# Changing when a routed-expert kernel loads weights and values, turns its pages, and drains GpSimd

## The chip, the cores and the metric

One core of one Trainium2 chip. The metric is device time in microseconds (us) of one execution. Lower is better. The kernel before takes 331.72 us (median of three runs, 329.25 to 331.78). A difference of 2% is 6.6 us.

Engine names in the profile: PE is TensorE, PEld its weight loads, DVE is VectorE, ACT is ScalarE, POOL is GpSimd, SP the engine that only issues DMAs. A "q" behind the name (POOLq) is that engine's sequencer.

## The reference, cut to what matters

```python
# attention: q, k, v are (8, 8, 576, 64); 128 random features; no softmax matrix
q_p, k_p = phi(q * scale), phi(k * scale)          # phi: projection, minus maximum, exp
num = einsum(q_p, einsum(k_p, v)); den = einsum(q_p, k_p.sum(seq)) + 1e-6
x = (num / den) -> (8, 576, 512)                   # 4608 tokens of 512
# experts: 8 of them, w1 (512 x 1024), w2 (1024 x 512); each token goes to one
e = argmax(x @ w_gate)  or the expert of the token before, by a local gate
out = softmax(x @ w_gate)[e] * (relu(x @ w1[e]) @ w2[e])
```

The tokens of one expert are gathered in pages of 128. There are 38 pages here: 18 for each half ("epoch") of the tokens and two overflow pages.

## The kernel before

Attention runs in 47 pipelined steps. 36 of them handle k, and q follows 11 steps behind. Then the gate makes the lists of tokens of epoch 0, and pages start while the lists of epoch 1 are made. A page is: gather (GpSimd, indirect DMA), turn (transposition, on TensorE or by DMA from SP), w1 matmul, relu, transposition of h, w2 matmul, scaling on VectorE, scatter (GpSimd, indirect DMA). The parts that the change touches:

```python
t_ = dict(k=kp4, v=kp2)[nm].tile(...)                   # two buffers for v
(nc.sync if nm == "v" else nc.gpsimd).dma_start(out=t_[:, :, c], in_=rows[nm][...])
...
def w_load():                                           # 64 loads of 256 KB, in order w1 then w2
    nc.gpsimd.dma_start(out=wdst[l][...], in_=src[e]...)
...
def turn(xg):      nc.sync.dma_start_transpose(out=xt, in_=xg)
def turn_pe(xg):   # four transposes on TensorE, one copy on ScalarE
...
def page(j, nw, gates):
    def mid():                                          # between the two halves of the w1 matmul
        if j + 1 < NEP:
            xts[j + 1] = turn_pe(xgs.pop(j + 1))
    ...  # hidden(j), transposition of h of page j - 1, gather of page j + 5
    if NEP <= j + 3 < NST:
        xts[j + 3] = turn(xgs.pop(j + 3))
    for _ in range(nw):
        w_load()
...
mo2 = pool("mo2", 4, **rw)                              # y: four results may wait for their scatter
```

From page 17 on, 1.5 results per page are multiplied by w2 and scattered.

The softmax here doesn't subtract the row's maximum and nothing guards it: scores larger than these inputs give would overflow.

Of the kernel before, what the change touches and what calls it, by code (L numbers as in the profile page):

```python
# [9 lines left out]
F32 = mybir.dt.float32  # L10
BF = mybir.dt.bfloat16
# [12 lines left out]
NEP = 18  # L24
# [6 lines left out]
def kernel(  # L31
# [12 lines left out]
    nc = tc.nc  # L44
    B, H, S, Dh = q.shape
    M, _ = omega.shape
    D, E = moe_w_gate.shape
    _, _, F = moe_w1.shape
# [3 lines left out]
    NP = B // 2  # L52
    DC, FC = D // 128, F // 128
# [10 lines left out]
    def pool(name, bufs, c=ctx, **kw):  # L64
        return c.enter_context(tc.tile_pool(name=name, bufs=bufs, **kw))
# [15 lines left out]
    kp1, kp2, kp3, kp4, kp6 = [pool("kp%d" % n, n, kctx, side="right") for n in (1, 2, 3, 4, 6)]  # L81
# [4 lines left out]
    LAG = 11  # L86
    NK = 9 * NP
# [5 lines left out]
    def load(P, nm, g):  # L93

        j0, nj = (8 * P, 8) if nm == "q" else (8 * P + 4 * g, 4)
        if nm == "q":
            t_ = arena.rearrange("p a x -> p (a x)").rearrange("p (w j x) -> p w j x", w=2, j=8)[:, P % 2]
        else:
            t_ = dict(k=kp4, v=kp2)[nm].tile([128, nj, 9 * Dh], F32 if nm == "v" else BF, name=nm + "s")
        cuts = [0, 4, 9] if (P, nm, g) == (0, "k", 0) else [0, 9]  # L100
        for c0, c1 in zip(cuts, cuts[1:]):
            c = slice(c0 * Dh, c1 * Dh)
            (nc.sync if nm == "v" else nc.gpsimd).dma_start(out=t_[:, :, c], in_=rows[nm][:, j0:j0 + nj, c])
        stg[P, nm, g] = t_
# [32 lines left out]
    def w_load():  # L137
        if wload and wdst[wload[0][0]] is not None:
            l, e, i = wload.pop(0)
            src = (moe_w1, moe_w2)[l]  # L140
            w = src.shape[2]
            nb = 1024 // w
            nc.gpsimd.dma_start(  # L143
                out=wdst[l][:, ds(e * WE + i * 1024, 1024)].rearrange("p (c f) -> p c f", f=w),
                in_=src[e].rearrange(("(c p) f -> p c f", "(p c) f -> p c f")[l], p=128)[:, i * nb:(i + 1) * nb, :])
# [222 lines left out]
    lists = {}  # L368
# [196 lines left out]
    pages, xgs, xts = [], {}, {}  # L565
# [27 lines left out]
    WH = 17  # L593
    outs, hs, done, spare = [], {}, [], list(range(3, 9))
    NST = 2 * NEP + 2

    def hidden(n, xt, ev_src, mid=lambda: None):
        ev = nc.values_load(ev_src, engines=(PE,), min_val=0, max_val=(E - 1) * WE,
# [12 lines left out]
    def hidden_t(h, n=FC):  # L611

        tp = ps_t.tile([128, FC, 128], BF, name="tp")
        for f in range(n):
            nc.tensor.transpose(tp[:, f], h[:, f], ident_bf)  # L615
        n_ = spare.pop(0) if spare else 0
        ht = arena[:, n_].rearrange("p (f c) -> p f c", c=128) if n_ else moh.tile([128, FC, 128], BF, name="ht")
        nc.vector.tensor_copy(ht[:, 0:n], tp[:, 0:n])  # L618
        if n < FC:
            nc.sync.dma_start_transpose(out=ht[:, n:], in_=h[:, n:].rearrange("p f c -> p (f c)"))  # L620
        return ht, n_
# [33 lines left out]
    def page(j, nw, gates):  # L655
        def mid():

            if j + 1 < NEP:
                xts[j + 1] = turn_pe(xgs.pop(j + 1))

        def gate_part():
            if gates:
                next(ga, None)

        if j < NST:
            hs[j] = hidden(j, xts.pop(j), pages[j][1], mid)
        gate_part()
        if j >= 1:
            h, ev = hs.pop(j - 1)
            done.append((pages[j - 1], hidden_t(h, FC // 2 if NEP <= j < NST - 1 else FC), ev))  # L670
        gate_part()
        if j + 5 == NEP:
            assert 1 in lists
            add_pages(1)
        if j + 6 == 2 * NEP:
            add_overflow()
        if j + 5 < NST:

            gs = pages[j + 5][0]
            xgs[j + 5] = fetch(gs[-1:], xgs.get(j + 5))  # L680
        if 2 * NEP <= j + 6 < NST:
            xgs[j + 6] = fetch(pages[j + 6][0][:1])
        if NEP <= j + 3 < NST:
            xts[j + 3] = turn(xgs.pop(j + 3))
        for _ in range(nw):
            w_load()


    todo = {}

    def at(t, *a):
        todo.setdefault(t, []).append(a)

    at(-1, load, 1, "k", 0)
    at(-1, load, 0, "q", 0)
    for P in range(NP):
        if P + 1 < NP:
            if P:
                at(9 * P - 5, load, P + 1, "k", 0)
            at(9 * P + 5, load, P + 1, "v", 0)  # L700
            at(9 * P - 1, load, P + 1, "k", 1)
            at(9 * P + 9, load, P + 1, "v", 1)
            at(9 * P + LAG + 1, load, P + 1, "q", 0)

    kvg, ga, early = [], None, [0, 0]
    gc = gate_consts()
# [17 lines left out]
    for t in range(NK + LAG + 3):  # L724
        s = t - LAG
        tk, tq, to = t < NK, 0 <= s < NK, 0 <= s - 2 < NK
        P, c = t // 9, t % 9

        slots(tk, tq)
        if tk:  # L730
            pe_kproj(t)
            dve_kmax(t)
        if tq:
            pe_qproj(s)
            act_qexp(s)
        if tk:
            act_kexp(t)
        if 0 <= s - 3 < NK:
            store_x(s - 3)
        if to:  # L740
            pe_o(s - 2)
        if t + 2 < NK + LAG:
            tp = pe_transposes(t + 2, s + 2)
        if t % 9 in (1, 6) and 6 <= t <= NK + 1:
            kvg.append(kv_pieces((t - 6) // 9, int(t % 9 == 1)))
        for g in list(kvg):
            if next(g, 1) == 1:
                kvg.remove(g)
        if to:
            dve_finish(s - 2)  # L750
        if t + 2 < NK + LAG:
            evac(t + 2, tp)
        if len(pages) > 0 and t > early[1] + 1:
            if early[0] == 0:
                xts[0] = turn_pe(xgs.pop(0))
            page(early[0], 1, False)
            early[0] += 1
        if ga is not None:
            next(ga, None)
            if next(ga, 1) == 1:  # L760
                ga = None

        if tk:
            pool_va(t)
        do(t)
        if t in (1, 3, 5, 7):
            next(gc, None)
        if tk:
            for _ in range(t > 8 and t % 5 in (0, 2, 4)):
                w_load()  # L770
        else:
            for _ in range(2 if 0 not in lists else 0):
                w_load()
        if t == NK + 1:

            kctx.close()
            w2_all = pool("w2p", 1, side="right", **rw).tile([128, E * WE], BF)
            wdst[1] = w2_all
            gt = pool("gt", 1, side="right", **rw)
            ga = both(0)  # L780
            next(ga)
        if 0 in lists and not pages:
            add_pages(0)
            early[1] = t
            for j in range(5):
                xgs[j] = fetch(pages[j][0])
# [8 lines left out]
    next(ga)  # L795
    for j in range(early[0], NST + 1):
        page(j, 3, True)
# [52 lines left out]
```

## Time and profile before

| stage | us from the start | what holds it |
|---|---|---|
| attention | 0 to about 110 | VectorE and ScalarE, with full DMA engines |
| lists of epoch 0 | 110 to 145 | small VectorE steps; TensorE partly at half clock |
| pages | 145 to 311 | TensorE |
| tail | 311 to 325.4 | nothing computes; GpSimd's bookkeeping and drain |

The profiled execution took 327.45 us, of which the trace spans 325.4. That is a fast one for this kernel: its 25 other timed executions in this study lie between 326.25 and 335.9 us (331.88 and 335.9 are marked slow: over 1.5% above the fastest of their kernel there). Where the record has the clock that TensorE was granted, the longer executions had less of it: on the chip of the third group 328.87 us at a mean of 0.944, 331.03 at 0.933 and 333.03 at 0.922. Which of the two brings about the other is not shown. Most lines that matter are in the prediction below. Two more matter for the result. The first fence holds the only wait of TensorE for k in the start of attention, then the v loads that SP issues in the first 30 us: start of the first, us from there to the end of the last, number. The third was issued at 24.4 us, because v had two buffers.

```profile
PE tp L168 <- DMA ks<-in_k_dram: 6.2, 1, 6.2
...
0.81 23.92 SPq L103 DMA_DIRECT2D vs<-in_v_dram  x3
```

And this is GpSimd from 60 to 120 us: us waited in total, times, longest. It sits idle for ScalarE (the exponential that it scales v by) 23.6 us and hardly ever for a weight.

```profile
POOL va L218 <- ACT ek L209: 23.6, 15, 3.0
POOL w_all L143 <- DMA w_all<-in_moe_w_dram: 1.5, 1, 1.5
```

### The profile page before, as it was taken

The numbers are of one execution on the slowest core, as the hardware profiler recorded it, in microseconds if no ns is written. First come the engines' busy times: TensorE is split into PE (matmuls) and PEld (weight loads), VectorE is DVE, ScalarE is ACT, GpSimd is POOL, SyncE is SP. The second block draws the span as 40 slices with busy tenths as digits, with TensorE's granted clock in tenths as the row PEclk, the third lists the DMA queues.
The fourth block names the chain that finished last, engine by engine and source line by source line (L and its number), as shares of the span: only waits on it lengthen the run. The fifth ranks groups of instructions, "written<-read, shape, count | busy, mean of one in ns | idle before, by whom it ended". The sixth has DMA issues, their size and how long they took to land. (4 is left out here: it accounts for less than half of the span.)

```text
span 325.4 us, 8102 instructions
## 1 busy us (share of the span) xinstructions
PE 254.3 (78%) x2949; PEld 152.8 (47%) x2969; DVE 180.1 (55%) x406; ACT 150.6 (46%) x227; POOL 175.8 (54%) x264
## 2 busy tenths in 40 slices
PE   0475788778688676576989897899999999999900
PEld 0353556556456464344555564444444444444400
DVE  4697498798798769923547753133333333334400
ACT  1177899898798874343555453211221122220000
POOL 8488585565545741536766663355555574334520
PEclk9999999999999778569999999999999999999985
DMA  7999989999979899829999999575686666322320
GB/s 239 232 208 269 268 137 280 280 251 285 271 187 179 162 218 229 216 50 192 176 215 225 226 226 185 121 184 171 174 191 164 161 177 174 114 91 105 120 82 0
DMA packets 52650, 60.48 MB, mean 186 GB/s; under 512 B 25552, under 2 KB 34768, under 8 KB 52608
## 3 DMA queue, kind: packets, MB, share of 16 engines
q0 software_dynamic: 23088, 40.58, 60.0%
q1 hardware_dynamic: 25440, 14.55, 16.8%
q10 hardware_dynamic: 4080, 4.77, 4.6%
q8 instruction: 28, 0.46, 0.6%
q14 instruction: 14, 0.11, 0.1%
HBM read 67.16 MB, written 14.68 MB: 251 GB/s over the span
## 5 line engine op out<-in xcount | busy, mean ns | idle before, releaser
L603 PE MATMUL pj<-w_all,xt 128*128 x293 | 74.2, 384 | 7.5 <-DMA xt<-xg 3.0
L608 ACT ACTIVATE arena<-pj 128x1024 bf16<-128x1024 f32 x38 | 38.9, 1024 | 78.0 <-PE pj L603 78.0
L634 POOL DMA_INDIRECT out_dram<-y,idr x38 | 37.8, 994 | 46.7 <-DVE y L633 45.1
L218 POOL TENSOR_TENSOR va<-vs,ek 128x512 bf16<-128x512 f32 (+1 forms) x40 | 38.1, 957 | 39.4 <-ACT ek L209 37.6
L574 POOL DMA_INDIRECT xg<-x_tok,ix x36 | 37.7, 1046 | 27.1 <-issue 7.6
L200 DVE TENSOR_REDUCE kmx<-pj 128x8 f32<-128x1024 f32 x36 | 44.0, 1222 | 12.5 <-ACT kvb L237 8.6
L143 POOL DMA_DIRECT2D w_all<-in_moe_w_dram x64 | 35.9, 567 | 19.6 <-DMA w_all<-in_moe_w_dram 14.7
L206 ACT ACTIVATE kp<-pj 128x1024 bf16<-128x1024 f32 x36 | 37.5, 1041 | 16.3 <-DVE kmx L200 16.3
L603 PEld LDWEIGHTS <-xt 128*128 128x128 bf16 x304 | 28.9, 99 | 32.9 <-DMA xt<-xg 2.7
L267 ACT ACTIVATE qp<-pj 128x1024 bf16<-128x1024 f32 x36 | 37.6, 1044 | 10.4 <-PE pj L261 10.4
L633 DVE TENSOR_SCALAR y<-po,prb 128x512 f32<-128x512 f32 x24 | 18.0, 751 | 28.9 <-PE po L628 28.9
L618 DVE COPY ht<-tp 128x1024 bf16<-128x1024 bf16 (+1 forms) x20 | 11.9, 596 | 26.2 <-PE tp L615 26.2
L291 DVE TENSOR_TENSOR xr<-po,rd 128x512 bf16<-128x512 f32 x36 | 24.9, 692 | 1.2
L194 PE MATMUL pj<-om_bd,kt 128*128 128x256 bf16 x144 | 22.4, 279 | 3.1 <-ACT kp L206 1.7
L628 PE MATMUL po<-w_all,ht 128*128 x102 | 24.5, 379 | 0.1
L168 PE MATMUL tp<-ident_bf,ks 128*128 128x128 bf16 x128 | 13.1, 228 | 12.9 <-DMA ks<-in_k_dram 6.2
L618 DVE COPY arena<-tp 128x512 bf16<-128x512 bf16 (+1 forms) x18 | 9.3, 514 | 24.7 <-PE tp L615 24.7
L628 PEld LDWEIGHTS <-ht 128*128 128x128 bf16 x160 | 15.1, 98 | 16.0
L713 ACT COPY qt<-tp 128x512 bf16<-128x512 bf16 x36 | 21.8, 605 | 1.5 <-DVE kt L711 1.4
L589 ACT COPY xt<-tp 128x512 bf16<-128x512 bf16 x18 | 10.5, 585 | 23.6 <-PE tp L587 22.3
L628 PE MATMUL po<-w_all,arena 128*128 x85 | 20.6, 379 | 0.2
L628 PEld LDWEIGHTS <-arena 128*128 128x128 bf16 x144 | 13.7, 98 | 14.9
(154 smaller groups left out, 373.7 us busy)
## 6 DMA issues: line engine op xcount, KB each, us to landing
w_all<-in_moe_w_dram POOLq DMA_DIRECT2D x64, 256.0 KB, 7.9
vs<-in_v_dram SPq DMA_DIRECT2D x8, 1152.0 KB, 9.2
arena<-in_q_dram POOLq DMA_DIRECT2D x4, 1152.0 KB, 11.9
x_tok<-xr ACTq DMA_DIRECT2D x16, 256.0 KB, 5.8
ks<-in_k_dram POOLq DMA_DIRECT2D x7, 576.0 KB, 12.6
out_dram<-y,idr POOLq DMA_INDIRECT x38, 2.8
xg<-x_tok,ix POOLq DMA_INDIRECT x36, 3.5
x_tok<-xr ACTq DMA_DIRECT2D x4, 128.0 KB, 6.2
```

What stands on the lines that cost most here:

```text
L143: nc.gpsimd.dma_start(out=wdst[l][:, ds(e * WE + i * 1024, 1024)].rearrange("p (c f) -> p c f", f=w), in_=src[e].rearrange(("(c p) f -> p ...
L194: nc.tensor.matmul(pj[:, 2 * i:2 * i + 2, :].rearrange("p a d -> p (a d)"), lhsT=kts[t][:, i], rhs=om_bd, start=True, stop=True)
L200: nc.vector.tensor_reduce(mx, kpj[t], axis=AX, op=Alu.max)
L206: nc.scalar.activation(kp, kpj.pop(t), Act.Exp, scale=scale)
L218: nc.gpsimd.tensor_tensor(va[:, x:x + 4 * n, 0:Dh].rearrange("p (h r) d -> p h r d", h=4), stg[P, "v", g].rearrange("p h (r d) -> p h r d" ...
L267: nc.scalar.activation(qp, qpj.pop(s), Act.Exp, scale=scale)
L291: nc.vector.tensor_tensor(xrs[s][:, u % 2, :].rearrange("p (g h d) -> p g h d", g=2, h=4), ov[:, :, :, 0:Dh], rd.to_broadcast([128, 2, 4, ...
L574: nc.gpsimd.indirect_dma_start(out=xg, out_offset=None, in_=src, in_offset=bass.IndirectOffsetOnAxis(ap=ix, axis=0), bounds_check=TE - 1, ...
L603: nc.tensor.matmul(h_ps[:, c, :], lhsT=xt[:, dc, :], rhs=w1_all[:, ds(ev + (dc * F + c * 512), 512)], start=(dc == 0), stop=(dc == DC - 1))
L608: nc.scalar.activation(h, h_ps.rearrange("p a x -> p (a x)").rearrange("p (c f) -> p f c", f=FC), Act.Relu)
L628: nc.tensor.matmul(y_ps[:, 0, :], lhsT=htn[0][:, f], rhs=w2_all[:, ds(ev + f * D, D)], start=(f == 0), stop=(f == FC - 1))
L634: s_ = nc.gpsimd.indirect_dma_start(out=out_flat, out_offset=bass.IndirectOffsetOnAxis(ap=idr[:, c:c + 1], axis=0), in_=y, in_offset=None, ...
```

## The change

Its intent: move most of GpSimd's final drain to a time at which nobody waits for GpSimd; have every w1 tile issued before the first page; let loads of v and q start earlier (the lines of k are written anew, but its loads stay in their steps); and keep the first three pages of epoch 1 away from late DMA transposes. Cut to its core:

```diff
-            t_ = dict(k=kp4, v=kp2)[nm].tile(...)
+            t_ = dict(k=kp4, v=kp3)[nm].tile(...)
...
+    NT = NEP + 3
-            if j + 1 < NEP:
+            if j + 1 < NT:                       # turn on TensorE
-    ... hidden_t(h, FC // 2 if NEP <= j < NST - 1 else FC)
+    ... hidden_t(h, FC // 2 if NT <= j < NST - 1 else FC)
-        if NEP <= j + 3 < NST:
+        if NT <= j + 3 < NST:                    # turn by DMA
...
         for _ in range(nw):
             w_load()
+        if j == NEP + 6:
+            nc.gpsimd.drain()
...
-            at(9 * P + 5, load, P + 1, "v", 0)       # and q likewise; k keeps its steps
+        at(max(9 * P - 9, 2), load, P, "v", 0)       # v 3 to 5 steps, q 3 steps earlier
...
-            page(early[0], 1, False)
+            page(early[0], 2, False)
-            for _ in range(t > 8 and t % 5 in (0, 2, 4)):
+            for _ in range(2 if t >= NK - 9 else t > 8 and t % 5 in (0, 2, 4)):
                 w_load()
-            for _ in range(2 if 0 not in lists else 0):
+            for _ in range(2 if t < 41 else 0):
                 w_load()
```

More of the change, by code (lines that the diff above doesn't have):

```diff
@@ L98, in load @@
         else:
-            t_ = dict(k=kp4, v=kp2)[nm].tile([128, nj, 9 * Dh], F32 if nm == "v" else BF, name=nm + "s")
+            t_ = dict(k=kp4, v=kp3)[nm].tile([128, nj, 9 * Dh], F32 if nm == "v" else BF, name=nm + "s")
         cuts = [0, 4, 9] if (P, nm, g) == (0, "k", 0) else [0, 9]
@@ L669, in page @@
             h, ev = hs.pop(j - 1)
-            done.append((pages[j - 1], hidden_t(h, FC // 2 if NEP <= j < NST - 1 else FC), ev))
+            done.append((pages[j - 1], hidden_t(h, FC // 2 if NT <= j < NST - 1 else FC), ev))
         gate_part()
@@ L695 @@
     at(-1, load, 0, "q", 0)
-    for P in range(NP):
-        if P + 1 < NP:
-            if P:
-                at(9 * P - 5, load, P + 1, "k", 0)
-            at(9 * P + 5, load, P + 1, "v", 0)
-            at(9 * P - 1, load, P + 1, "k", 1)
-            at(9 * P + 9, load, P + 1, "v", 1)
-            at(9 * P + LAG + 1, load, P + 1, "q", 0)
+    for P in range(1, NP):
+        if P > 1:
+            at(9 * P - 14, load, P, "k", 0)
+        at(max(9 * P - 9, 2), load, P, "v", 0)
+        at(9 * P - 10, load, P, "k", 1)
+        at(9 * P - 4, load, P, "v", 1)
+        at(9 * P + LAG - 11, load, P, "q", 0)
     kvg, ga, early = [], None, [0, 0]
```

## The prediction

> **What bounds the kernel now.** I read the page first, then the table by stretches, the waits of TensorE by stretch, the timeline where TensorE's busy share dips, and last the rows of the closing lines, because the page's chain of waits holds two short pieces at 311 us and says nothing of the 13 us after them. From the page:
>
> ```profile
> span 325.4 us, 8102 instructions
> ...
> PE 254.3 (78%) x2949; PEld 152.8 (47%) x2969; DVE 180.1 (55%) x406; ACT 150.6 (46%) x227; POOL 175.8 (54%) x264
> ...
> PE   0475788778688676576989897899999999999900
> ...
> PEclk9999999999999778569999999999999999999985
> DMA  7999989999979899829999999575686666322320
> ```
>
> One slice is 8.1 us. The run has four stages with different limits; the stretches (sum and busy times in us, then clock, DMA share, GB/s) show them:
>
> ```profile
> 60.00:70.00 10.00, 8.40 (x198) 6.29 (x199) 8.16 (x18) 8.87 (x16) 5.51 (x9) 1.00 1.12 275
> 90.00:100.00 10.00, 8.21 (x154) 5.92 (x155) 9.83 (x21) 9.89 (x17) 5.69 (x10) 1.00 0.73 160
> 130.00:140.00 10.00, 5.50 (x72) 3.52 (x66) 8.44 (x34) 4.20 (x6) 5.43 (x6) 0.50 0.78 192
> 200.00:210.00 10.00, 6.99 (x45) 3.61 (x44) 2.46 (x7) 2.05 (x2) 1.69 (x2) 1.00 0.65 115
> 250.00:260.00 10.00, 9.95 (x53) 4.80 (x53) 3.85 (x6) 2.05 (x2) 5.38 (x6) 1.00 0.60 162
> 310.00:325.00 15.00, 0.00 (x0) 0.00 (x0) 0.64 (x1) 0.00 (x0) 1.15 (x2) 0.67 0.09 31
> ```
>
> Attention (to 110 us) is held by VectorE and ScalarE together (0.8 to 1.0 each), with the DMA engines full most of the time. The gate's lists (110 to 145) are a chain of small VectorE steps with TensorE half idle at half clock. The pages (150 to 310) are TensorE's, above 0.95 but for one hole at 200. After 311 no engine computes. The waits on DMA that reach TensorE after the start are few (us in total, times, longest); the first line is from the stretch 60 to 110, the others from the whole run:
>
> ```profile
> PE tp L171 <- DMA arena<-in_q_dram: 1.3, 1, 1.3
> ...
> PE pj L603 <- DMA xt<-xg: 3.0, 1, 3.0
> ...
> PE pj L603 <- DMA w_all<-in_moe_w_dram: 2.2, 1, 2.2
> ```
>
> The hole at 200 in the timeline, and then the rows of the lines that end the program (shortest/median/longest in ns, first and last start):
>
> ```profile
> 196.22 7.25 SPq L581 DMA_TRANSPOSE xt<-xg  x3
> ...
> 204.41 1.89 PE L603 MATMUL pj<-w_all,xt 128*128 x8 [3.01 <-DMA xt<-xg]
> ```
>
> ```profile
> L811 POOLq INC_SWDGE_SEM  x1: 2150/2150/2150, 314.3 to 314.3; - x1
> ...
> L845 POOLq DRAIN  x3: 51/103/8069, 316.5 to 325.1; - x3
> ...
> L845 ACTq DRAIN  x2: 8/8/8, 292.9 to 324.8; - x2
> ```
>
> The last scatter is issued at 310.9 and has landed at 314.2. Then GpSimd takes 2.15 us for a bookkeeping instruction and, from 316.5, 8.07 us for a drain while every other engine waits at the final barrier. That drain is the largest single wait in the run, and it does no work.
>
> **What the Trainium skill says.** "Perfetto Trace Analysis", section "Sequencer-only Instruction (DRAIN, etc)": such an instruction's reported time is its execution alone, without the wait on semaphores. So the 8.07 us are not a wait for the scatter; the trace agrees, since the scatter landed 2.3 us before. "VectorE: DVE Perf Modes", section "The DRAIN you can't avoid": the boilerplate drains take about 12 ns on all five engines. The trace agrees for four (ScalarE 8 ns) and not for GpSimd. "DMA: Bandwidth & Descriptors", section "SWDGE vs HWDGE vs iDMA": GpSimd's cores write descriptors for its own DMAs into rings, and SP and ScalarE do not go through them. My inference, which no page states, is that GpSimd's drain retires the entries of all its DMAs since the drain before. The first one, at 0.4 us with no DMA behind it, took 184 ns. The same page, "Issuing engines are not separate DMA queues": all queues share the 16 DMA engines, so an earlier v load takes from k and q.
>
> **The change part by part.**
>
> Drain. GpSimd issued 155 DMAs: 64 weights, 9 k, 4 q, 40 gathers, 38 scatters. 8.07 us over 155 is 52 ns each. The new drain stands in page 24 after the gather for page 29. By the loop's rule 9 scatters are issued before it, so 29 scatters and 10 gathers (6 pages and two overflow pages with two each) remain: 39 entries, 2.0 us. The tail loses 6.0 us. The new drain must take about 116 entries, 6 us, plus 3 us for the gather still in flight. In the pages GpSimd is half idle (5.4 of 10 us); a result comes each 3 us, y has four buffers, so three results can wait 9 to 12 us; gathers run five pages (4.5 us each) ahead. Cost on the path: none. The 2.15 us of bookkeeping may have the same cause; I take half, 1.0 us.
>
> Pages 18 to 20. Taken away: the 3.0 us hole, which comes because GpSimd, behind on weights until 193.9, gathers page 18 late and three transposes by DMA follow. Added on TensorE: per page four transposes of x and four more of h, each group 0.22 us between matmuls (the trace's 0.61 us for eight against 0.39 for four): 3 x 0.44 = 1.3. Net 1.7 us less. ScalarE's three copies (0.59 each) fit in its idle time.
>
> w1 complete. Before, two w1 loads follow pages 0 and 1, and page 1 waits 2.2 us for one. By counting the steps, in the new kernel all 32 are issued by step 37, the lists come at step 43. Gain 2.2 us. It isn't free: 28 instead of 16 w1 loads are issued by step 35. Near 117 to 135 us they land 1.4 us apart, so 12 more want 17 us of DMA before about 107 us. GpSimd waits for the load eight back, so eight in flight (11 us) cost nothing, and some 3 us of DMA idle at 90 to 100 can be used. 3 us remain as waits of GpSimd ahead of its scaling of v, which the kv matmuls need; half may be hidden: plus 1.5. Six w2 loads now stand ahead of the first gathers in GpSimd's queue: plus 1.0.
>
> v and q earlier. Step 27 loses the wait on q (1.1 of the 1.3 us). The v waits were 0.7 us on GpSimd and hidden. But the third v load has now a free buffer and starts at once instead of at 24.4 us, beside k and q of the start; the second k group landed at 15.6 and is needed at 17.0; 1152 KB ahead of it cost some 3 us at the rate of that stage, of which I count 1.0.
>
> Sum: -6.0 -1.0 -1.7 -2.2 -1.1 +1.0 +1.5 +1.0 = -8.5 us. On 331.7 that is 323.2.
>
> **The rivals.**
>
> A: the drain has a fixed cost. Then the tail keeps its 8 us and the page stage holds a second one; only 2.5 us are gained, about 329. The 184 ns of the first drain and the 51 and 103 ns of the last two speak against it; that no drain in this trace follows a middle number of DMAs leaves it open.
>
> B: DMA becomes the bound of attention. With the share at 1.1 from 50 to 90 us, 12 more weight loads push the kv matmuls, and through TensorE's order all later steps, by 6 us or more; the lists slip with them. About 328. For it: the full DMA rows. Against: in the saturated stretch the loads already took 10 to 17 us to land and GpSimd never waited for one before 110 us.
>
> C: the drain stalls the pages: the scatters back up, VectorE has no y, TensorE stops for some us. Then the gain in the tail is given back, about 326. GpSimd's idle time speaks against it.
>
> D: everything hides, the bookkeeping shrinks too and the clock is granted earlier, because TensorE is fed better around 145 us: 318 or less. Half clock lasted from about 127 to 145 us in this trace.
>
> **Range and chances.** Sum of sure parts (tail, hole, w1 wait): -9.9; of unsure costs: +3.5, less 2.1. Rival A or B alone leaves a gain under 2% (6.6 us); I give them together about 30%. The runs before spread over 2.5 us. So 323.2 us, 317 to 329 in 8 of 10; faster by over 2%: 0.66; within 2%: 0.31; slower: 0.03.
>
> **What would show it.** In the new profile: the last GpSimd drain near 2 us and a new one near 6 to 9 us in the pages at about 235 to 245 us, with TensorE's slices still at 9; the wait of pj on xt gone; the wait of pj on w_all gone; the wait on q at step 27 gone; GpSimd waiting for weights between 85 and 115 us, a few us in all; step 36 at 107 us, give or take 3. The prediction is wrong if the last drain keeps its 8 us (A), if the steps from 27 on stretch (B), if TensorE has a hole after the new drain (C), or if the start of attention slips by more than 2 us on k.

## The result, and the profile after

The changed kernel is correct and took 319.14 us (median of four runs, 319.03 to 319.35), beside 331.75 us for the kernel before in the runs made with it (four runs, 329.25 to 332.88). The ratio is 0.9631, with a 95% interval of 0.9576 to 0.9685: faster. Ratios here are the mean time of one kernel's fast runs over that of the other's of the same rounds, so not quite the ratio of the medians quoted.

The page of the changed kernel, answering to the rows that the prediction shows of before:

```profile
span 317.3 us, 8143 instructions
...
PE 255.9 (81%) x2973; PEld 153.8 (48%) x2993; DVE 180.5 (57%) x406; ACT 152.5 (48%) x230; POOL 175.5 (55%) x264
...
PE   0276778787877765849989979999999999999970
...
PEclk9999999999999999556999999999999999999996
DMA  7999999999979999979999931146746866631330
```

TensorE does slightly more work (255.9 us for 254.3). Its empty slices at the end shrink from two to one, and where the hole was (a 7 and an 8 in slices 25 and 26) stand two 9s. The DMA row falls to 1 in these slices, for the weights are done by then.

Two stretches and the waits of TensorE on DMA in the whole run (columns as before):

```profile
200.00:210.00 10.00, 9.95 (x70) 5.54 (x70) 3.58 (x5) 4.24 (x5) 2.08 (x2) 1.00 0.27 67
250.00:260.00 10.00, 9.95 (x53) 4.76 (x52) 3.65 (x9) 2.12 (x3) 6.13 (x6) 1.00 0.68 186
```

```profile
PE tp L168 <- DMA ks<-in_k_dram: 8.6, 2, 7.0
...
PE tp L587 <- DMA xg<-x_tok,ix: 0.2, 1, 0.2
```

The three waits that the prediction named (q, w1, turned page) are gone. The stretch with the hole went from 6.99 to 9.95 us busy. The wait on k, though, has become two waits and 2.4 us longer. The closing rows, with the new drain first (shortest/median/longest in ns, first and last start):

```profile
L690 POOLq DRAIN  x1: 6862/6862/6862, 230.5 to 230.5; - x1
L814 POOLq INC_SWDGE_SEM  x1: 970/970/970, 312.2 to 312.2; - x1
...
L848 POOLq DRAIN  x3: 51/103/3234, 313.2 to 317.0; - x3
```

The last drain fell from 8.07 to 3.23 us, the bookkeeping from 2.15 to 0.97 us: 6.0 us of the tail. The new drain's 6.86 us show on GpSimd's timeline (start, us, then the idle time before it):

```profile
230.14 0.99 POOL L635 DMA_INDIRECT out_dram<-y,idr  x1 [0.71 <-DMA xt<-xg]
231.44 1.05 POOL L574 DMA_INDIRECT xg<-x_tok,ix  x1 [0.31 <-issue]
238.24 1.01 POOL L635 DMA_INDIRECT out_dram<-y,idr  x1 [5.75 <-issue]
```

There is a pause of 5.75 us, and afterwards scatters and gathers come back to back until 251 us. TensorE has no wait between 200 and 310 us, and its stretches stay at 9.95 busy.

Where the time went, as differences of the two profiled executions (after minus before, us from each start; steps by VectorE's row maximum, pages by ScalarE's relu):

| point | before | after | difference |
|---|---|---|---|
| step 3 | 18.5 | 21.3 | +2.8 |
| step 27 | 81.9 | 84.7 | +2.8 |
| step 28 (q wait gone) | 85.5 | 87.7 | +2.2 |
| step 35 | 106.6 | 108.8 | +2.2 |
| page 0 | 144.8 | 146.0 | +1.2 |
| page 1 (w1 wait gone) | 150.9 | 150.0 | -0.9 |
| page 17 | 201.1 | 200.3 | -0.8 |
| page 18 (hole gone) | 206.4 | 202.7 | -3.7 |
| page 21 (added turns) | 219.1 | 216.4 | -2.7 |
| page 37 | 291.8 | 289.0 | -2.8 |
| end of span | 325.4 | 317.3 | -8.1 |

The two traces differ by 8.1 us, the medians by 12.6 us. Of the missing 4.5 us, 4.3 are the difference between the profiled execution of before and its median (331.75 less 327.45). The changed kernel's profiled execution (319.12) is typical of its runs. No trace of a slower execution of before was taken here, so these 4.3 us are not assigned to any part.

### The profile page after: what moved, and what is told of

Its sections match the earlier page's. It is cut to its first block, busy times and chain, and to the rows that moved or that the text cites. A ratio compares the mean times of both kernels' runs of the same rounds, so it can differ in the third digit from the quotient of the medians.

```text
span 317.3 us, 8143 instructions
## 1 busy us (share of the span) xinstructions
PE 255.9 (81%) x2973; PEld 153.8 (48%) x2993; DVE 180.5 (57%) x406; ACT 152.5 (48%) x230; POOL 175.5 (55%) x264
## 5 line engine op out<-in xcount | busy, mean ns | idle before, releaser
L609 ACT ACTIVATE arena<-pj 128x1024 bf16<-128x1024 f32 x38 | 38.9, 1024 | 70.7 <-PE pj L604 68.0
L218 POOL TENSOR_TENSOR va<-vs,ek 128x512 bf16<-128x512 f32 (+1 forms) x40 | 38.2, 958 | 34.1 <-ACT ek L209 33.9
L194 PE MATMUL pj<-om_bd,kt 128*128 128x256 bf16 x144 | 23.4, 288 | 2.5 <-ACT kp L206 0.7
L589 ACT COPY xt<-tp 128x512 bf16<-128x512 bf16 x21 | 12.3, 585 | 25.5 <-PE tp L587 24.3
L629 PEld LDWEIGHTS <-arena 128*128 128x128 bf16 x144 | 13.7, 98 | 14.9
```

The source lines that it names most:

```text
L194: nc.tensor.matmul(pj[:, 2 * i:2 * i + 2, :].rearrange("p a d -> p (a d)"), lhsT=kts[t][:, i], rhs=om_bd, start=True, stop=True)
L218: nc.gpsimd.tensor_tensor(va[:, x:x + 4 * n, 0:Dh].rearrange("p (h r) d -> p h r d", h=4), stg[P, "v", g].rearrange("p h (r d) -> p h r d" ...
L609: nc.scalar.activation(h, h_ps.rearrange("p a x -> p (a x)").rearrange("p (c f) -> p f c", f=FC), Act.Relu)
L629: nc.tensor.matmul(y_ps[:, 0, :], lhsT=htn[0][:, f], rhs=w2_all[:, ds(ev + f * D, D)], start=(f == 0), stop=(f == FC - 1))
```

## The experiments

Twelve kernels ran, in three groups, each group on one chip beside its own runs of before: 328.62 us in the first (seven runs, 326.25 to 331.88), 331.98 us in the second (330.36 to 332.98), 332.4 us in the third (328.87 to 335.9). Each kernel gave correct results. Unless said otherwise, an edit is made to the changed kernel. The chip of the first measurement is not on record, and the changed kernel itself ran again in the third group alone. So where a kernel of the first two groups is set beside the changed kernel, a microsecond or two between their times shows nothing by itself; the readings below rest on stages of the traces. Stages that an edit leaves alone agree well: pages 24 to 37 take 58.16 us in the four traces of the first group and in the first two.

### First group: one part undone at a time

**No drain.**

```diff
-        if j == NEP + 6:
-            nc.gpsimd.drain()
```

> The changed kernel without the drain in the pages, all else kept. Theory (GpSimd's drain retires the entries of its DMAs since the drain before, and in the pages this is hidden): the last drain is back at 8.0 to 8.2 us instead of 3.2 and the bookkeeping instruction at about 2.1 instead of 1.0, the pages are unchanged; about 324.5 us against 319.1 of the changed kernel (5.4 more). Rival A (a fixed cost of a drain): 319 or less, last drain near 3.2 us. Rival C (the drain stalls the pages): pages end earlier than 308 us and the total is under 324.

Measured: 326.36 us (325.6 to 326.42), ratio 0.9932. The closing rows of this kernel:

```profile
L811 POOLq INC_SWDGE_SEM  x1: 2150/2150/2150, 313.1 to 313.1; - x1
...
L845 POOLq DRAIN  x3: 51/103/8069, 315.2 to 323.9; - x3
```

To the nanosecond these are the two long rows of before, though weights, loads and turns are the new ones. The span is 324.1, 6.8 us over the changed kernel's, of which 0.8 already stood at page 37. The other 6.0 are the tail. In the pages nothing changed: pages 30 to 37 take 30.9 us with the drain and without. So the drain's cost is moved, not fixed, and where it was moved to it cost nothing. Rival A of the prediction falls. This run also shows how little the rest of the change is worth: all of it together took 1.3 us off the span (325.4 to 324.1 in these two traces), and the times class as the same as before.

**Old loads of v and q, two v buffers.**

```diff
-            t_ = dict(k=kp4, v=kp3)[nm].tile(...)
+            t_ = dict(k=kp4, v=kp2)[nm].tile(...)      # and the old schedule of the loads
```

> The changed kernel with two v buffers and the old times of all q, k, v loads; weights, drain and TensorE turns kept. Theory (the third v load, which now starts at once, takes the DMA engines from the first k groups): steps 0 to 5 are 2.8 us earlier again, the wait on q at step 27 (0.6 us net) is back; about 317 us, 2 less than the changed kernel. Rival B (the 12 more w1 loads need the earlier q and v loads to be out of the way): GpSimd and the kv matmuls wait for weights or q from step 27 on, 320 us or more.

Measured: 320.0 us (318.58 to 320.82), ratio 0.974; span 317.7. A miss. Step 3 came at 18.3 us, 3.0 earlier than in the changed kernel, and TensorE's wait on k was one of 6.0 us as in before. So the longer start is the load part's doing. But page 0 came at 146.1, where the changed kernel has 146.0: the lead was lost on the way. Its waits and clock say where. The wait on q (1.1 us) is back at step 28, and TensorE's clock was halved from 33.1 to 36.5 us and from 111.6 to 118.4 us, which the changed kernel's trace does not have. Here is the later stretch in this kernel; the clock is the third number from the end of the line:

```profile
110.00:120.00 10.00, 7.50 (x177) 5.59 (x177) 5.99 (x21) 7.07 (x14) 5.07 (x10) 0.66 1.11 232
```

**Old weight schedule.**

```diff
-            page(early[0], 2, False)
+            page(early[0], 1, False)
-            for _ in range(2 if t >= NK - 9 else t > 8 and t % 5 in (0, 2, 4)):
+            for _ in range(t > 8 and t % 5 in (0, 2, 4)):
-            for _ in range(2 if t < 41 else 0):
+            for _ in range(2 if 0 not in lists else 0):
```

> The changed kernel with the old pace of the weight loads (two w1 loads left after the first pages); loads, drain and TensorE turns kept. Theory (page 1 waits 2.2 us for a w1 load, and that is all): 321 to 322 us. Rival (the timed runs of the kernel before are 2 to 5 us longer than its profiled one, those of the changed kernel are not; the leftover w1 loads are what varies, with TensorE's clock hanging on that wait): 323 to 326 us, with a spread of over 1 us between runs, where the changed kernel has 0.3.

Measured: 322.15 us (321.45 to 324.18), ratio 0.9832; span 319.7, 2.4 over the changed kernel's. Page 0 is at 146.4, page 1 at 152.2 instead of 150.0, and from there the delay stays at 2.2 to 2.6. TensorE's wait for w1 is back, and nothing else of its waits on weights:

```profile
PE pj L604 <- DMA w_all<-in_moe_w_dram: 2.0, 1, 2.0
```

The spread of 2.7 us that the rival asks for is there too, but the kernel with the old loads, which has no w1 wait, spreads by 2.2, so it singles out nothing.

**Pages 18 to 20 turned by DMA.**

```diff
-    NT = NEP + 3
+    NT = NEP
```

> The changed kernel with pages 18 to 20 turned by DMA as before; loads, weights and drain kept. Theory as predicted (the hole of 3.0 us at page 18 comes from the transposes by DMA at the change of method, the added TensorE work is 1.3 us): hole back, about 321 us. Rival: the hole came from GpSimd's backlog of weights up to 194 us; with the weights done near 185 us the gathers are early and the transposes land in time, so the hole stays away and the kernel is 1.3 us faster than the changed one, 317.8 us.

Measured: 318.42 us (317.91 to 319.45), ratio 0.9701; span 316.5. The hole at page 18 did not come back: page 17 to 18 takes 200.4 to 202.6 us, and the stretch from 195 to 205 is full.

```profile
195.00:205.00 10.00, 9.95 (x72) 5.77 (x71) 4.00 (x10) 3.89 (x5) 0.83 (x1) 1.00 0.37 79
205.00:215.00 10.00, 9.95 (x53) 4.81 (x53) 3.36 (x6) 2.05 (x2) 5.52 (x6) 1.00 0.67 169
```

From page 16 to page 21 (page 17 already holds the first of the added turns) this kernel takes 17.9 us and the changed one 19.4. So with the new weight schedule the turns on TensorE only cost 1.5 us, near the 1.3 of the prediction, and the hole had gone for another reason. The trace names it: GpSimd issued its last weight at 178.1 us here and at 193.9 in before, gathered page 18 at 185.0 and 189.0, and SP's first transposition, which waits for that gather to land, started at 188.2 and 196.2 (in before, the line is in the prediction):

```profile
188.24 10.41 SPq L581 DMA_TRANSPOSE xt<-xg  x3
```

### Second group: parts alone and combined

**The drain alone, in the kernel before.**

```diff
+        if j == NEP + 6:
+            nc.gpsimd.drain()
```

> The kernel before with the drain in page 24 and nothing else of the change. Theory: the last drain goes from 8.07 to 3.2 us and the bookkeeping from 2.15 to 0.97, six us less than the kernel before of the same rounds, pages unchanged; ratio about 0.982. Rival (the drain pays only together with the earlier weights, since GpSimd is behind on them up to 194 us in the kernel before): a hole on TensorE near 240 us and a ratio above 0.99.

Measured: 325.72 us (322.95 to 328.25), ratio 0.9842 (0.9772 to 0.9913): 6.3 us by the medians, where the theory has 6.0 in the tail. One of the four runs, 328.25 us, is marked slow, and the ratio can be reproduced only with it counted in. The two long drains are the changed kernel's, 6861 and 3234 ns, so the tail lost its 6.0 us. But pages 24 to 37 took 59.8 us in this trace instead of 58.2 (the holes discussed below), and the interval, some 3 to 8 us, cannot tell whether these 1.6 us are in the gain or not. It also reaches across 2%, so the gain is shown and "over 2%" is not. The rival, a ratio above 0.99, falls.

**The third v load issued later, from ScalarE's queue in step 2.**

```diff
-            (nc.sync if nm == "v" else nc.gpsimd).dma_start(...)
+            (nc.scalar if (P, nm, g) == (1, "v", 0) else
+             nc.sync if nm == "v" else nc.gpsimd).dma_start(...)
```

In the changed kernel's program this load stands at step 2 already, but SP has nothing else to wait for, and with a third buffer free it issues the load at once. ScalarE is held back by its own work.

> The changed kernel with one edit: the third v load is issued from ScalarE's queue, which reaches it in step 2 near 19 us, and not from SP's at the start. Theory (that load at the start costs 2.8 us of k): step 5 is at 21.4 us again instead of 24.3. What of it is left at the end is what the run shows: 316.4 us if all of it is, 319 if the stage of the lists takes it back as it did in the run with the old loads (step 5 there 2.9 us earlier, page 0 at the same time, half clock for 6.8 us at 112 us and 3.4 at 33). Rival: the load lands too late for step 9 and steps 9 to 15 stretch.

Measured: 323.41 us (320.57 to 325.3), ratio 0.9745. In time a miss: 316.4 to 319 was expected, from traces of other chips. In the start it is as expected. The load now starts at 19.2 us, TensorE waits on k once (6.8 us), and step 5 is at 22.8 us; the next experiment, which has the changed kernel's loads, has it at 25.0 on the same chip. So 2.2 us of the start are caused by that one load. At page 0 the lead was 1.5 us; half clock from 35.4 to 38.9 us stands between. Pages 30 to 37 took 32.5 us instead of 30.9, with holes in TensorE that no run of the first group has. More on that below.

**Old weights and DMA turns together, with the drain and the new loads.** The edits are the third and the fourth of the first group.

> The changed kernel with both the old pace of weights and the transposes by DMA of pages 18 to 20. With the run of old weights alone (TensorE turns kept: no hole) it completes a table of two by two. Theory now (the hole at page 18 is GpSimd's backlog of weights): the hole of about 3 us is back, because the weights again end near 194 us, and this kernel is 1.5 to 2 us slower than the one with old weights and TensorE turns (322.2): about 324 us. Rival (the hole is the start of the DMA transposes as such): there would be one in the run with new weights and DMA turns, and there was none; then no hole here either and about 321 us.

Measured: 329.39 us (327.79 to 330.95), ratio 0.9919, 5 us more than expected. Beside the trace with old weights alone this one is 8.4 us longer: 2.8 at page 0, 3.3 in pages 16 to 21, and 2.2 in pages 24 to 37; of these only pages 16 to 21 belong to the edit. The hole is back, in the same size as in before; this is TensorE's timeline (start, us, then the idle time ahead and what ended it):

```profile
208.84 2.52 PE L604 MATMUL pj<-w_all,xt 128*128 x8 [3.00 <-DMA xt<-xg]
```

Page 17 to 18 takes 205.5 to 211.5 us, and half clock from 210.0 to 213.4 follows. With the runs above this makes a table of four:

| | old weights | new weights |
|---|---|---|
| pages 18 to 20 turned by DMA | hole of 3.0 us (before, and this run); under 1 us in the drain-alone run | none |
| turned on TensorE | none | none |

Either part alone takes the hole away. It comes from GpSimd being behind on weights when it should gather page 18, and it is close to the edge: the drain-alone kernel has the same two old parts and shows only a small one (page 17 to 18 in 3.2 us). There page 17 itself came 1.6 us later than in before (202.7 for 201.1) and the gather of page 18 0.4 us later (189.4 for 189.0), which is why little of the lateness could show.

**Three drains, with the later v load and DMA turns.**

```diff
-        if j == NEP + 6:
+        if j in (NEP + 2, NEP + 10, NEP + 15):
```

> A candidate: third v load from ScalarE's queue, pages 18 to 20 turned by DMA, and three drains, in pages 20, 28 and 33, instead of one. It also measures the drain: 16 entries are left for the last one. If a drain costs 1.6 us plus 42 ns for each entry (the line through 155 entries in 8.07 us and 39 in 3.23), the last takes 2.2 us and the bookkeeping 0.7; if it costs 52 ns an entry without a fixed part, as I predicted, 0.8 us. With the line: 318.4 of the run with DMA turns, less 1.3 in the tail, less 0 to 2.8 at the start: 314.3 to 317 us. Rival: the two added drains hold scatters back when three results come in 9 us, TensorE gets holes after 250 us, and the gain is given back.

Measured: 322.48 us (321.65 to 323.19), ratio 0.9717. A miss: 314 to 317 was expected. The last drain fell to 1351 ns, between the two prices expected, and the bookkeeping to 520, together 2.3 us less than in the changed kernel. But TensorE has holes now. Two stretches of ten microseconds (busy time of TensorE is the number after the length):

```profile
230.00:240.00 10.00, 8.97 (x49) 4.26 (x47) 2.99 (x6) 3.07 (x3) 5.09 (x5) 1.00 0.62 162
...
260.00:270.00 10.00, 8.01 (x44) 3.86 (x43) 2.75 (x8) 2.05 (x2) 6.32 (x7) 1.00 0.70 138
```

The gain of the tail was given back in the pages. Whether the drains did that was open, because the three other kernels of this group, with one drain, had holes too. That was what the third group was for. The three drains in the pages took, shortest, median and longest in ns:

```profile
L690 POOLq DRAIN  x3: 4876/5892/6044, 213.9 to 276.9; - x3
```

The longest is the first of the three. The other two are far longer than their few DMAs would have them; the part on the prediction comes back to this.

### Third group: a better version, and the changed kernel again

**The later v load, DMA turns, one drain in page 24.** The edits are those of the later-v-load and DMA-turns kernels.

> The changed kernel with two edits that the earlier runs favour: the third v load from ScalarE's queue in step 2, and the DMA turns of the pages from 18 on. One drain in page 24 as in the changed kernel. From the parts measured so far: start 1.5 us less at page 0, turns 1.0 us less, so about 2.5 us under the changed kernel on the same chip. Theory (scatters back up behind the drain and the four y buffers run out): if pages 30 to 37 take 32 us and not 30.9, TensorE must show waits for y in the stretch 240 to 290 us, and then only about 1 us is gained. Rival (slower pages are a matter of the chip, not of y): the pages stretch without such waits, or in the changed kernel's own run on this chip just as much.

Measured: 322.38 us (321.74 to 323.56), ratio 0.9754. It is 1.6 us under the fast runs of the changed kernel on the same chip (last run of this group), of 2.5 expected. Pages 30 to 37 took 33.0 us, and between 240 and 290 us TensorE waited 1.5 us for y, in two waits.

**As that, with w2 matmuls from page 13 on and eight y buffers.**

```diff
-    WH = 17
+    WH = 13
-    mo2 = pool("mo2", 4, **rw)
+    mo2 = pool("mo2", 8, **rw)
```

> As the run before, but the output matmuls begin at page 13 in place of 17 (the weights are complete by then) and y has eight buffers in place of four; the room comes from the transposed h, which needs fewer buffers. About nine more scatters stand ahead of the drain, so about 30 entries after it: at 83 ns each 2.5 us for the last drain in place of 3.2, bookkeeping 0.8. Theory (y buffers and backlog): no wait of TensorE for y after the drain, pages 30 to 37 in 31 us or less, 1 us or more under the run before. Rival: the same holes remain, because they are landings of gathers and not of scatters; then no gain but 0.7 us.

Measured: 323.45 us (322.31 to 325.01), ratio 0.979: 1.1 us more, where 1 less was expected. Pages 30 to 37 still took 32.2 us, and TensorE still waited for VectorE's instruction that makes y and so frees the matmul's result (1.5 us in three waits). The trace puts none of VectorE's waits there on a scatter. So a backlog of scatters in too few y buffers does not explain the holes; that theory falls.

**As that, with the drain in page 31.**

```diff
-        if j == NEP + 6:
+        if j == NEP + 13:
```

> As the run before with the drain seven pages later, in page 31, after nearly all gathers: about 12 entries remain. By 83 ns each the last drain takes 1.0 us and the bookkeeping about 0.45 us, 2 us less in the tail than the run before. The drain in the pages takes 8 to 9 us (143 entries); with eight y buffers and one result each 3 us it should stall nothing. Expected 2 us under the run before. Rival (the drain costs the pages something wherever it stands late): TensorE waits for y in the stretch behind it and the gain is under 0.5 us.

Measured: 319.91 us (317.62 to 320.99), ratio 0.9656 (0.9561 to 0.9751). It is the fastest of this group: 3.5 us under the kernel that differs only in the drain's place, 4.1 us under the fast runs of the changed kernel beside it. Closing rows of the two, first with the drain in page 24, then in page 31:

```profile
L690 POOLq DRAIN  x1: 7334/7334/7334, 240.8 to 240.8; - x1
L814 POOLq INC_SWDGE_SEM  x1: 850/850/850, 315.9 to 315.9; - x1
...
L848 POOLq DRAIN  x3: 51/103/2744, 316.8 to 320.1; - x3
```

```profile
L690 POOLq DRAIN  x1: 8911/8911/8911, 274.2 to 274.2; - x1
L814 POOLq INC_SWDGE_SEM  x1: 480/480/480, 315.3 to 315.3; - x1
...
L848 POOLq DRAIN  x3: 51/103/1192, 315.8 to 317.6; - x3
```

1.6 us less for the drain and 0.4 less for the bookkeeping: the 2 us expected. Of the remaining 1.5 us, 1.1 are in the traces between pages 24 and 30, the pages that follow the drain in the one kernel and precede it in the other: 28.4 us against 27.2. The intervals of the two ratios overlap, so the extra is seen in one trace each, not established.

**The changed kernel, unaltered.**

> The changed kernel unaltered, on the chip of the three runs before, so that they can be compared with it. Expected ratio to the kernel before 0.963, as first measured; 30.9 us for pages 30 to 37 if the longer pages of two earlier experiments came from those kernels, 32 us or more if they came from their chip.

Measured: 324.04 us (median of five; four fast ones 323.69 to 324.1, one of 329.13 us in the slow state), ratio 0.9787 (0.9708 to 0.9867), not 0.963: faster, but whether by 2% is unclear. Its profile is of the slow execution (pages 30 to 37 in 35.0 us, half clock from 275.0 to 278.4 us), so it cannot answer what was asked of these pages, and only its parts that need no comparison of times are used. The last drain and the bookkeeping take the same 3234 and 970 ns as on the first chip.

### What the holes on two of the chips are, as far as it goes

All the kernels of the second and third group have them, and none of the first group's, nor the first two traces of before and after: where these take 58.16 us for pages 24 to 37, the seven fast traces of the other two groups take 59.7 to 61.4. This is VectorE in the better version with one drain, then in the changed kernel of the first measurement, at the same pages (start, us, then the idle time ahead and what ended it):

```profile
241.97 0.75 DVE L634 TENSOR_SCALAR y<-po,prb 128x512 f32<-128x512 f32 x1 [1.30 <-PE po L629]
246.37 0.43 DVE L619 COPY ht<-tp 128x512 bf16<-128x512 bf16 x1 [3.64 <-PE po L629]
248.74 0.75 DVE L634 TENSOR_SCALAR y<-po,prb 128x512 f32<-128x512 f32 x1 [1.95 <-PE pj L629]
249.41 0.74 DVE L634 TENSOR_SCALAR y<-pj,prb 128x512 f32<-128x512 f32 x1
```

```profile
241.87 0.75 DVE L634 TENSOR_SCALAR y<-po,prb 128x512 f32<-128x512 f32 x1 [1.30 <-remote]
243.82 0.42 DVE L619 COPY ht<-tp 128x512 bf16<-128x512 bf16 x1 [1.20 <-PE tp L616]
245.55 0.75 DVE L634 TENSOR_SCALAR y<-po,prb 128x512 f32<-128x512 f32 x1 [1.30 <-PE po L629]
247.27 0.75 DVE L634 TENSOR_SCALAR y<-pj,prb 128x512 f32<-128x512 f32 x1 [0.98 <-PE pj L629]
```

The copy of h waits only for TensorE's transposes, and those are in place in both traces: here is TensorE in the better version, going on without a pause.

```profile
243.50 0.39 PE L616 MATMUL tp<-ident_bf,arena 128*128 128x128 bf16 x4
243.72 1.89 PE L629 MATMUL po<-w_all,ht 128*128 x8
```

Yet VectorE starts at 246.37 instead of 243.9. Its next instruction is late too, at 248.74, and the one after follows without a pause. The trace holds TensorE's semaphore update for these transposes at 246.34, and the next ones bunched between 248.71 and 249.30. So the word that TensorE was done came late, by 2.5 us here and by up to 5.2 us elsewhere (earlier outputs with the drain in page 24; 6.0 in the slow execution), and ScalarE's relu was late in the same way, by up to 1.6 us. The Trainium skill, "Perfetto Trace Analysis", section "Tensor Engine Instruction (MATMUL, LD_WEIGHTS)", says that the end of a matmul in the profile is a model, and that the semaphore update follows PSUM's acknowledgement and its propagation. So these records cannot tell whether the matmuls or only their updates were late.

Such a delay needs no drain in the pages. All eight traces of these two chips have one of 2.0 to 2.7 us between 140 and 147 us, in the stage of the lists, and none of the other six has. Here is TensorE, then VectorE, in the better version with one drain, 88 us ahead of that drain; the update for these matmuls stands in the trace at 142.10, where their records end at 139.4:

```profile
138.69 0.71 PE L277 MATMUL po<-kvb,qp 128*64 128x74 bf16 x16
...
142.12 0.21 DVE L290 RECIPROCAL rd<-po 128x8 f32<-128x8 f32 x1 [3.40 <-remote]
```

So part of it belongs to these chips, or to the sessions on them, and not to the change. The way from step 35 to page 0, in which this falls, took 39.0 us or more there and 37.2 to 38.6 in the other six traces.

What part the drain has in it is open. For it: in the pages, all delays of more than 2.2 us but one come after the first drain there. And the place of the loss moves with the drain. The two kernels with earlier outputs differ in the drain's place alone: with the drain in page 31, pages 28 to 34 take the 27.24 us of the first group, with the drain in page 24 they take 29.35. With a first drain in page 20, page 22 is the first to lose. Against it, besides the delay among the lists: the first delay with the drain in page 31 belongs to transposes recorded at 272.3 us, while the drain is recorded from 274.2; and in the first measurement and the first group the same drain has none of this. A kernel without a drain, profiled on one of these two chips, would tell; none was. The kernel before was about equally fast on all the chips, to about 1%; the changed kernel's fast runs took 1.5% longer on the third chip than at first.

## Why the prediction was right or wrong

The verdict (faster by over 2%) and the range held in the first measurement: 319.14 us in 317 to 329, 4.1 us under the point. The gain was 12.6 us by the medians and 8.1 in the traces; the prediction said 8.5. On the third chip the medians of the fast runs are 323.97 us beside 331.72, a gain of 7.7 us, and there "over 2%" is not shown. Of the four signs by which the prediction said it would be wrong, one came true: the start of attention slipped by more than 2 us on k (2.8 us at step 3, with the wait on k 2.4 us longer). Of its signs of being right, the last drain near 2 us failed; it took 3.2. By its own terms:

**The drain (-6.0, with the bookkeeping -1.0): direction right, size off.** Measured -4.8 and -1.2, together 6.0 of 7.0. The mis-sized term is the price of one entry: the prediction divided 8.07 us evenly over 155 DMAs. The runs separate the kinds. Entries are GpSimd's DMAs since its drain before, counted in each trace and in the program's order: the DMA that stands just ahead of a drain in the program counts as before it, though the record of the drain begins first.

| drain | indirect | direct | measured ns | 49 + 81.7 x indirect + 21.4 x direct |
|---|---|---|---|---|
| last, before | 78 | 77 | 8069 | 8069 |
| last, changed kernel | 39 | 0 | 3234 | 3235 |
| last, earlier outputs | 33 | 0 | 2744 | 2745 |
| last, three drains | 16 | 0 | 1351 | 1356 |
| last, late drain | 14 | 0 | 1192 | 1193 |

The three constants are estimates, worked out from three of the rows (before, changed kernel, late drain); the other two rows test them. So the prediction had the 39 entries right, and one costs 82 ns and not 52. That they lie in rings, as the page cited there has it, no run here shows. Four drains in the pages fit too. The changed kernel's record of 6862 ns begins 1.97 us before the gather that is ahead of it in the program has ended (231.44 to 232.48). What is left is 4.89 us, and the sum for 39 indirect and 77 direct is 4.88. The first of three drains leaves 4.08 us (sum 4.07), the drain in page 24 with earlier outputs 5.38 (5.37), the drain in page 31 6.93 (6.93).

The second and the third of three drains do not fit. They have 20 and 13 indirect DMAs behind them, 1.68 and 1.11 us by the sum, and took 2.91 and 4.66 us from the end of the DMA ahead of them. By the trace's semaphores that DMA's data landed at 255.46 and at 282.22 us, and the drains ended at 256.31 and 282.79. So it looks as if a drain also ends only after the data in flight has landed; in the changed kernel that had happened long before (at 234.48, for a drain that ended at 237.38), and the entries decided. Two cases suggest it and no experiment tests it. The 3 us that the prediction added for a gather in flight may thus be a real wait, but in the changed kernel only the 1.97 us until GpSimd was done with the gather stand in its place. The bookkeeping instruction follows the entries as well: 480, 520, 850, 970 and 2150 ns in the order of the table from below. That a drain amid the pages costs nothing on the path is shown in the first group and in the first measurement: no wait of TensorE, 30.9 us for pages 30 to 37 with and without. Rival C did not happen there. On the two other chips TensorE does have holes after the drain, but not as C has it: the traces put no wait of VectorE or TensorE there on a scatter.

**The hole (-3.0, +1.3): sum right, cause wrong.** The prediction let the TensorE turns take the hole away. The new weight schedule takes it away by itself, as the DMA-turns kernel shows. The turns on TensorE are then a cost of about 1.5 us with no return. From page 16 to 21 the changed kernel gained 1.6 us on before, of 1.7 predicted.

**w1 complete (-2.2): right.** Page 0 to page 1 gained 2.1 us, and undoing it brought 2.0 us of wait back.

**Waits for weights in attention (+1.5): wrong, nothing.** GpSimd did wait for weights, 4.3 us in five waits from 60 to 120 us. But its waits for ScalarE shrank from 23.6 to 16.3 us, and from step 28 to 35 the difference of the two kernels stays at 2.2. The waits went into idle time that was there before:

```profile
POOL va L218 <- ACT ek L209: 16.3, 14, 2.3
POOL w_all L143 <- DMA w_all<-in_moe_w_dram: 4.3, 5, 1.4
```

Rival B falls with it.

**w2 loads ahead of the gathers (+1.0): not separated.** Page 0's lag fell from 2.2 to 1.2 us on the way there. Before had half clock from 110.3 to 117.2 us and the changed kernel did not, which hides what the loads cost, if anything.

**v at the start (+1.0) and q (-1.1): the first too small by 1.8, the second too large by 0.5.** The mechanism was named, and the later-v-load kernel shows it by giving 2.2 us back at step 5; that agrees with the page on shared DMA engines that the prediction cites. The third v load is issued at once:

```profile
0.81 26.76 SPq L103 DMA_DIRECT2D vs<-in_v_dram  x4
```

The delay begins with the first step, which differs by 0.8 us, and it is no matter of luck: step 5 came at 23.8 to 25.0 us in the six traces with the early load, and at 21.2 to 22.8 in the eight without. That q gained 0.6 instead of 1.1 fits the old-loads kernel, where the wait is 1.1 long and costs 0.5 to 0.6 of step time.

**What the prediction missed.** The clock, which it has in rival D alone. Its half-rate stretches up to page 0 fall differently from run to run. In all traces, leaving out the one at the end that the program's end cuts off, they last 3.4, 6.8, 10.2, 13.7, 17 or 20.5 us, which are multiples of 3.4. The Trainium skill, "TensorE: Matmul & The Clock Gate", section "Part 1: The HAM clock gate", states a free-running window of 3413 ns and a clock that is either full or half; the traces agree with the length and with the two values, and whether the window runs freely no run here tests. In the six traces of the first measurement and the first group, the way from step 35 to page 0 took 38.2 to 38.6 us where such a stretch of 6.8 us lay between 110 and 119 us, and 37.2 to 37.3 where none or one of 3.4 did. That is 0.8 to 1.4 us, as much as several of the predicted terms. That the half clock is the cause and not a sign of a TensorE that waits is argued here, not shown. With the change of chip it is a likely reason why undoing one part whose worth is 1 or 2 us did not show up as such in the time, in the old-loads run above all.

**Ledger of the profiled pair:** start +2.8, q -0.6, clock and lists -1.0, w1 -2.1, hole and turns -1.9 (pages 17 to 21), tail -5.4 (of which the drain and bookkeeping are 6.0, less a last scatter that landed later). That is -8.2 us beside the 8.1 of the spans. The point was near for the traces partly by luck: the drain's entries, v and q came out worse than predicted by 1.2, 1.8 and 0.5 us, the waits for weights, the w2 loads and the clock better. By the medians the gain was 4.1 us larger, and that rests on the slower executions of before that no trace explains.

## What to carry to other kernels

A wait at the very end of a program, after the last engine computes, is worth looking at first: here an instruction that does no work held the end for 8 us, its cost grew with the number of DMAs issued before it, and paying it early, as late as the engine still has idle time, took 6 us off the end (on two other chips some of that was lost again in the pages after it). When a prefetch gets one more buffer, ask what will now start at once and what urgent load it will stand beside. And undo each part of a change by itself before keeping it: one part here was credited with a hole that another part removes as well, and beside that other part it only cost 1.5 us.

## What the Trainium skill lacked or had wrong

- "VectorE: DVE Perf Modes", section "The DRAIN you can't avoid", gives about 12 ns for the boilerplate drains on all five engines. GpSimd's last one took 8069 ns in the kernel before, and 1192 to 3234 ns where another drain had come before it in the pages.
- No page looked up for this case says that GpSimd's drain takes longer the more DMAs GpSimd has issued since the last one: about 82 ns for an indirect and 21 ns for a direct one here, and 51 to 184 ns with none. Nor that with few entries it may last until the DMA ahead has landed (ended at 256.31 us after a landing at 255.46, at 282.79 after 282.22).
- No page has the INC_SWDGE_SEM instruction at the end: 2150 ns with 78 indirect and 77 direct DMAs before it, 970 with 39 indirect, 480 with 14.
- "Perfetto Trace Analysis", section "Sequencer-only Instruction (DRAIN, etc)", gives the reported time as execution alone. The drain in page 24 is recorded from 230.51 us, though the gather ahead of it in the program ran from 231.44 to 232.48 on the same engine: 1.97 of its 6.86 us pass until that gather has ended.
- No page looked up says that TensorE's semaphore updates can reach other engines 2 to 5 us after its records end, as they did on two of the chips here (246.34 us for transposes recorded at 243.50 to 243.89).
